# Reordering one step of a hand-scheduled pipeline: later multiply-adds, an earlier seed, the sigmoid at the front

## The chip, the core and the metric

The kernel runs on one core of a Trainium2 chip. The metric is the device time of one execution in microseconds. Most executions of one kernel agree within 0.3%; where a ratio to the kernel before is given, the runs of both were made on the same chip in the same rounds. Two experiments set side by side can come from different rounds.

## The reference, cut to what matters

```python
X = np.fft.fft(x, axis=1)                 # x: (8, 3136, 256)
X = np.fft.fft(X, axis=2).real            # the attention block
h = np.maximum(X @ w_in, 0.0)             # w_in: (256, 1024)
conv = sum(conv_w[k] * shifted(h, k) for k in range(3))   # along the sequence; cut
out = (h * 1 / (1 + np.exp(-conv))) @ w_out               # w_out: (1024, 256)
```

The kernel turns the Fourier transform into matrix products with tables and uses symmetry, so that the columns of one half of a sequence give both halves. While one batch goes through the second part ("the steps"), the next batch's transform runs beside it, cut into pieces and hung on the steps.

## The kernel before

The second part has 8 batches × 4 chunks of columns × 8 blocks of 128 features = 256 steps. The matrix products write tiles in PSUM, the other tiles of a step lie in SBUF; both are memories of the core. One step's parts, with the engine on which each runs:

```python
def seed(s):                      # ScalarE: pa starts from a scaled row
    pa[s] = psa.tile(...)         # 2 PSUM buffers
    act(pa[s][:, 0:n], eb[b, c], AF.Copy, scale=ge[:, f:f + 1])

def products(s):                  # TensorE
    pb[s] = psb.tile(...)         # 1 PSUM buffer
    mm(pb[s][:, 0:n], G[0:P - 1, 1, fs], PQ[b][1][...], True, True)
    mm(pa[s][:, 0:n], G[:, 0, fs], PQ[b][0][...], False, True)

def combine(s):                   # twice: ScalarE copies pb scaled by 1 or -1, VectorE adds it to pa
    ...
        act(nb[:, i, cols], p[:, cols], AF.Copy, scale=-1.0 if i else 1.0)        # L485
        nc.vector._custom_dve(TENSOR_ADD_SAT, out=to, in0=a[:, cols],             # L486
                              in1=nb[:, i, cols], s0=BIG, s1=0.0)

def first_tap(s):                 # ScalarE, L492
    act(gs[s], hs[s][:, 0:n], AF.Copy, scale=cw[:, 0, s[2]:s[2] + 1])

def other_taps(s):                # VectorE, L498: two multiply-adds
    for k in (1, 2):
        stt(out=g, in0=h[:, k:k + n], scalar=cw[:, k, f:f + 1], in1=g, op0=ALU.mult, op1=ALU.add)

def sigmoid(s):                   # ScalarE, L501
    act(gs[s], gs[s], AF.Sigmoid)

def gate(s):                      # half GpSimd (L508), half VectorE (L509)
    m = n // 2
    gt(g[:, m:n], g[:, m:n], h[:, m + 1:n + 1], op=ALU.mult)
    vt(g[:, 0:m], g[:, 0:m], h[:, 1:m + 1], op=ALU.mult)
```

The schedule is written by hand. Every engine is given its own instructions in the order in which this loop issues them:

```python
LAG = 3
for t in range(n + LAG):
    run("act")                    # copies of the next batch's transform
    if t < n:
        products(steps[t])
        combine(steps[t])
    if 0 <= t - 2 < n:
        gate(steps[t - 2])
    run("load")
    if 0 <= t - 1 < n:
        sigmoid(steps[t - 1])
    run("dve")                    # the next batch's transform on VectorE
    if t < n:
        first_tap(steps[t])
        other_taps(steps[t])
    if t + 1 < n:
        seed(steps[t + 1])
    if t >= LAG:
        mm2(steps[t - LAG])       # TensorE; every eighth step also the output copies on ScalarE
    run("pe")
```

## Time and profile before

| | kernel before |
|---|---|
| median of the runs | 1336.1 us |
| TensorE / VectorE / ScalarE / GpSimd busy | 91% / 88% / 66% / 35% |

Two engines are near their limits, and the work of a step goes round between four engines. Such a profile is read from the timeline of one step: for each idle stretch, which instruction ended it, and what stood in front of that instruction on its own engine. The prediction below shows those lines. In lines of the profile PE is TensorE (PEld its loading of weights), DVE is VectorE, ACT ScalarE and POOL GpSimd, and L158 is line 158 of the kernel.

### The profile page before, as it was taken

The page shows a single profiled execution, that of the slowest core. Times are in us where ns is not written, and L with a number is a line of the kernel's source. Part 1 is how long each engine was busy: PE and PEld are TensorE (multiplying, and loading weights), DVE is VectorE, ACT ScalarE, POOL GpSimd, SP SyncE. Part 2 cuts the span into 40 slices and gives each one's busy share as a digit, 9 for nine tenths or more (in the row PEclk, how much of TensorE's full clock was granted, in tenths as well). Part 3 has the DMA queues.
Part 4 walks back from the last instruction along what each step waited for, and adds up shares of the span by engine and source line. Part 5 has one row for each costly group of instructions (what it writes and reads, how often), then busy time and mean ns, then how long its engine had stood idle before and what let it go on. Part 6 is the DMA issues. An engine that isn't in the chain of part 4 may idle for free.

```text
span 1334.3 us, 15340 instructions
## 1 busy us (share of the span) xinstructions
PE 1214.4 (91%) x4914; PEld 892.2 (67%) x4914; DVE 1175.9 (88%) x1664; ACT 887.0 (66%) x1558; POOL 462.1 (35%) x507
## 2 busy tenths in 40 slices
PE   0748899989899999999999999999999999999998
PEld 0425677767676777777676777767677777776766
DVE  6969999998998999998999899999899888878885
ACT  0225666667666677776767777776777767777775
POOL 2415525242532435242523335242332223222222
PEclk9968999999999999999999999999999999999999
DMA  7601202021120102120102102120001000100001
GB/s 227 176 25 37 85 25 65 32 64 35 54 67 24 52 26 71 49 75 25 60 13 74 50 25 73 48 75 0 25 24 48 27 24 25 34 30 22 24 20 43
DMA packets 46840, 66.02 MB, mean 49 GB/s; under 512 B 5600, under 2 KB 35196, under 8 KB 46504
## 3 DMA queue, kind: packets, MB, share of 16 engines
q1 hardware_dynamic: 41012, 49.80, 11.8%
q0 software_dynamic: 5120, 12.85, 3.2%
q10 hardware_dynamic: 628, 2.40, 0.6%
q8 instruction: 38, 0.62, 0.2%
q14 instruction: 42, 0.34, 0.1%
HBM read 39.24 MB, written 25.74 MB: 49 GB/s over the span
## 4 chain that ended last, share of the span: by engine, by line
DVE 50%; PE 22%; ACT 12%; issue 12%; DMA 3%; POOL 1%; DVEq 0%; ACTq 0%; POOLq 0%; SPq 0%
DVE g L498 16%; DVE h L486 15%; PE po L89 11%; ACT g L492 6%; PE pd L89 4%; DVE g L509 4%; PE pa L89 4%; PE pb L89 4%; DVE xh L158 3%; ACT os L525 2%; DVE xh L147 2%; DVE w L174 2%; DMA out_dram<-os 1%; ACT nb L485 1%; ACT pa L466 1%
## 5 line engine op out<-in xcount | busy, mean ns | idle before, releaser
L89 PE MATMUL po<-wout,g 128*128 128x256 f32 (+2 forms) x3200 | 735.9, 380 | 0.7 <-POOL g L508 0.7
L89 PEld LDWEIGHTS po<-wout,g 128*128 128x128 f32 (+2 forms) x3200 | 602.9, 188 | 149.1 <-issue 19.0
L498 DVE SCALAR_TENSOR_TENSOR g<-h,cw,g 128x770 f32<-128x770 f32 (+2 forms) x512 | 537.1, 1049 | 82.0 <-ACT g L492 72.3
L508 POOL TENSOR_TENSOR g<-g,h 128x385 f32<-128x385 f32 (+1 forms) x256 | 295.0, 1152 | 776.9 <-ACT g L501 634.1
L485 ACT ACTIVATE nb<-pb 128x386 f32<-128x386 f32 (+4 forms) x512 | 227.6, 499 | 147.2 <-PE pb L89 145.8
L501 ACT ACTIVATE g<-g 128x770 f32<-128x770 f32 (+2 forms) x256 | 221.1, 864 | 149.1 <-DVE g L498 148.6
L486 DVE CUSTOM_DVE_ANT_0 h<-pa,nb 128x386 f32<-128x386 f32 (+4 forms) x512 | 265.7, 561 | 50.4 <-PE pa L89 31.9
L492 ACT ACTIVATE g<-h,cw 128x770 f32<-128x770 f32 (+2 forms) x256 | 243.6, 952 | 46.9 <-DVE h L486 30.3
L89 PE MATMUL pa<-pt,G 128*128 128x386 f32 (+2 forms) x512 | 223.7, 518 | 43.8 <-ACT pa L466 43.6
L89 PE MATMUL pb<-qt,G 127*128 127x386 f32 (+2 forms) x512 | 215.8, 502 | 1.6 <-ACT nb L485 1.5
L89 PEld LDWEIGHTS pa<-pt,G 128*128 128x128 f32 x512 | 91.0, 191 | 144.7 <-ACT pa L466 101.4
L509 DVE TENSOR_TENSOR g<-g,h 128x385 f32<-128x385 f32 (+2 forms) x256 | 155.0, 606 | 0.5 <-ACT g L501 0.5
L466 ACT ACTIVATE pa<-eb,ge 128x386 f32<-128x386 f32 (+2 forms) x256 | 146.9, 574 | 8.1 <-DMA eb<-ed 8.1
L89 PE MATMUL pd<-tab,w 99*128 99x196 f32 (+2 forms) x448 | 123.1, 381 | 17.7 <-ACT g L492 6.1
L89 PEld LDWEIGHTS pb<-qt,G 127*128 127x128 f32 x512 | 94.7, 192 | 27.6 <-issue 4.5
L89 PEld LDWEIGHTS pd<-tab,w 99*128 99x128 f32 (+1 forms) x448 | 80.0, 189 | 44.7 <-ACT g L492 24.2
L122 POOL DMA_INDIRECT xh<-in_x_dram,idx x64 | 85.3, 1333 | 16.4 <-issue 12.2
L525 ACT COPY os<-po 128x256 f32<-128x256 f32 (+2 forms) x200 | 58.4, 384 | 13.5 <-DMA out_dram<-os 8.8
L158 DVE TENSOR_TENSOR xh<-xh 98x1024 f32<-98x1024 f32 (+1 forms) x32 | 51.1, 1603 | 0.1
L147 DVE TENSOR_TENSOR xh<-xh 98x1020 f32<-98x1020 f32 (+1 forms) x32 | 46.6, 1466 | 0.0
L89 PE MATMUL po<-win,dm 128*128 128x512 f32 x8 | 5.7, 872 | 38.9 <-DMA dm<-dft_dim_dram 38.9
L174 DVE TENSOR_TENSOR w<-xh 98x508 f32<-98x508 f32 (+1 forms) x32 | 37.5, 1172 | 0.1
(84 smaller groups left out, 352.8 us busy)
## 6 DMA issues: line engine op xcount, KB each, us to landing
out_dram<-os SPq DMA_DIRECT2D x184, 128.0 KB
xh<-in_x_dram SPq DMA_DIRECT2D x16, 784.0 KB
eb<-ed SPq DMA_DIRECT2D x16, 193.0 KB
tab<-dft_seq_dram SPq DMA_DIRECT2D x4, 601.8 KB
raw<-in_moe_w_in_dram ACTq DMA_DIRECT2D x2, 1024.0 KB
raw<-in_moe_w_out_dram SPq DMA_DIRECT2D x1, 2048.0 KB
eb<-ed SPq DMA_DIRECT2D x8, 209.0 KB
eb<-ed SPq DMA_DIRECT2D x8, 192.5 KB
```

Source lines behind the costliest of these rows:

```text
L89: nc.tensor.matmul(o, l, r, start=start, stop=stop, skip_group_check=True)
L122: nc.gpsimd.indirect_dma_start(out=xh[b, h][0:NP, 4 + m].rearrange("p q d -> p (q d)"), out_offset=None, in_=bass.AP(tensor=x.tensor, offs ...
L158: vt(flat(to, to + 2), flat(0, 2), flat(2, 4), op=op)
L466: act(pa[s][:, 0:n], eb[b, c], AF.Copy, scale=ge[:, f:f + 1])
L485: act(nb[:, i, cols], p[:, cols], AF.Copy, scale=-1.0 if i else 1.0)
L486: nc.vector._custom_dve(TENSOR_ADD_SAT, out=to, in0=a[:, cols], in1=nb[:, i, cols], s0=BIG, s1=0.0)
L492: act(gs[s], hs[s][:, 0:n], AF.Copy, scale=cw[:, 0, s[2]:s[2] + 1])
L498: stt(out=g, in0=h[:, k:k + n], scalar=cw[:, k, f:f + 1], in1=g, op0=ALU.mult, op1=ALU.add)
L501: act(gs[s], gs[s], AF.Sigmoid)
L508: gt(g[:, m:n], g[:, m:n], h[:, m + 1:n + 1], op=ALU.mult)
L509: vt(g[:, 0:m], g[:, 0:m], h[:, 1:m + 1], op=ALU.mult)
L525: nc.scalar.copy(out=osb[0:m, j % 2], in_=pt[0:m, j % 2])
```

## The change

The intent is to take the wait for the first tap off VectorE: the multiply-adds of a step are put off to the next step, when their tap is long done. The sigmoid then comes a step later too, and the change puts it at the very front of the step.

```diff
         run("act")
+        if 0 <= t - 2 < n:
+            sigmoid(steps[t - 2])
         if t < n:
             products(steps[t])
             combine(steps[t])
+        if t + 1 < n:
+            seed(steps[t + 1])
+        if t < n:
+            first_tap(steps[t])
         if 0 <= t - 2 < n:
             gate(steps[t - 2])
         run("load")
+        run("dve")
         if 0 <= t - 1 < n:
-            sigmoid(steps[t - 1])
-        run("dve")
-        if t < n:
-            first_tap(steps[t])
-            other_taps(steps[t])
-        if t + 1 < n:
-            seed(steps[t + 1])
+            other_taps(steps[t - 1])
         if t >= LAG:
             mm2(steps[t - LAG])
```

## The prediction

> **What bounds the kernel now.** The kernel computes 256 steps: 8 batches, 4 chunks of columns, 8 blocks of features. One step t makes `products` (TensorE), `combine` (ScalarE scales and copies `pb` into `nb`, VectorE adds it to `pa`, twice), `first_tap` (ScalarE), two multiply-adds `other_taps` (VectorE), and, in later steps, `sigmoid` (ScalarE), `gate` (half VectorE, half GpSimd) and `mm2` (TensorE). The schedule is written by hand: each engine takes its instructions in the order of the text, so what matters is who waits for whom around one step. I read the busy shares first, then the work of each engine in stretches, then VectorE's list of waits, then the timeline of one step.
>
> The page's busy shares, and the windows (first data row: batches 0 to 6 with their transform of the next batch beside them; second: the last batch alone):
>
> ```profile
> PE 1214.4 (91%) x4914; PEld 892.2 (67%) x4914; DVE 1175.9 (88%) x1664; ACT 887.0 (66%) x1558; POOL 462.1 (35%) x507
> ```
>
> ```profile
> core 0: us, PE busy (x) PEld busy (x) DVE busy (x) ACT busy (x) POOL busy (x), PEclk, DMA share, GB/s
> 90.40:1186.00 1095.60, 1038.03 (x4216) 765.66 (x4215) 997.07 (x1385) 764.47 (x1344) 396.09 (x424) 0.99 0.14 43
> 1186.00:1318.50 132.50, 129.74 (x512) 94.07 (x512) 108.91 (x156) 104.05 (x181) 36.04 (x37) 1.00 0.08 25
> ```
>
> TensorE and VectorE run near their limits together. The first add of the steps starts at 90.4 us and the last step's at 1318.5, so 255 steps take 1228.1 us, 4.82 each; VectorE is busy for 997.07 + 108.91 = 1106.0 of it and idle for 122.1, or 0.48 a step. No rearrangement of VectorE's waits can therefore gain more than 122 us (9%), and TensorE, with 1167.8 of the 1228.1 busy, would stop it well before. VectorE's waits, in the list of who waited for whom:
>
> ```profile
> DVE g L498 <- ACT g L492: 72.3, 119, 0.9
> DVE h L486 <- PE pa L89: 31.9, 45, 9.6
> DVE h L486 <- ACT nb L485: 18.0, 25, 2.1
> ```
>
> The change aims at the first: multiply-adds (L498) waiting for the first tap (L492). The timeline of one undisturbed step of the last batch, VectorE and then ScalarE (start, duration, instruction, idle before):
>
> ```profile
> 1212.09 1.02 DVE L498 SCALAR_TENSOR_TENSOR g<-h,cw,g 128x769 f32<-128x769 f32 x1
> 1213.03 1.02 DVE L486 CUSTOM_DVE_ANT_0 h<-pa,nb 128x385 f32<-128x385 f32 x2
> 1213.96 0.55 DVE L509 TENSOR_TENSOR g<-g,h 128x384 f32<-128x384 f32 x1
> 1215.11 2.08 DVE L498 SCALAR_TENSOR_TENSOR g<-h,cw,g 128x769 f32<-128x769 f32 x2 [0.60 <-ACT g L492]
> 1217.11 0.55 DVE L486 CUSTOM_DVE_ANT_0 h<-pa,nb 128x385 f32<-128x385 f32 x1
> ```
>
> ```profile
> 1213.15 0.85 ACT L501 ACTIVATE g<-g 128x769 f32<-128x769 f32 x1 [0.64 <-DVE g L498]
> 1214.14 0.94 ACT L492 ACTIVATE g<-h,cw 128x769 f32<-128x769 f32 x1
> 1214.98 0.57 ACT L466 ACTIVATE pa<-eb,ge 128x385 f32<-128x385 f32 x1
> 1215.71 0.87 ACT L485 ACTIVATE nb<-pb 128x385 f32<-128x385 f32 x2 [0.16 <-PE pb L89]
> 1217.22 0.85 ACT L501 ACTIVATE g<-g 128x769 f32<-128x769 f32 x1 [0.64 <-DVE g L498]
> ```
>
> The step is 1217.11 − 1213.03 = 4.08 us. Read the order on ScalarE: the two scaled copies (1215.71) come before the sigmoid (1217.22). So the next adds find `nb` ready and start the moment the multiply-adds end, while the sigmoid, which also waits for those multiply-adds, runs beside the adds. VectorE's only idle time is the 0.60 before the multiply-adds.
>
> **What the Trainium skill says.** "Perfetto Trace Analysis", section "Tensor Engine Instruction": "ACT/DVE/GPSIMD are strict FIFO". The trace agrees: the seed at 1214.98 reads only `eb` and `ge`, which had long been there, and still starts only behind the tap. "ScalarE: Activation LUTs", section "What ACT_TABLE_LOAD costs": an activation takes 186 ns + 0.833 ns an element, 93 more for a pointer operand, and neighbours overlap by about 93. For the sigmoid of 769 that gives 827 ns, against 850 here; tap and seed overlap by 1214.14 + 0.94 − 1214.98 = 0.10. The same page, section "Table sets: the hidden batching unit", says that cheap functions lie in every set. The by-shape groups agree: L501 has a single table load in the whole run, although copies and sigmoids alternate, so the moved sigmoid adds none.
>
> **The change part by part.** No instruction is added or removed; the same 256 of each kind are put in another order.
>
> *Multiply-adds one step later.* In step t VectorE now does adds(t), gate(t−2), transform work if there is some, multiply-adds(t−1). Their tap was made a step earlier, so the wait for it goes. In the step above the multiply-adds start at once behind the gate, 0.47 after its start (two neighbours on VectorE overlap by 0.08) in place of 1.15 (1215.11 − 1213.96): −0.68.
>
> *Sigmoid(t−2) first on ScalarE.* Its input is now the output of multiply-adds(t−2), which VectorE finishes as the **last** thing of step t−1. Behind it in the same FIFO stand the scaled copies of step t, without which VectorE can't start adds(t). This closes a ring: multiply-adds end → sigmoid → first scaled copy → adds. VectorE has nothing else to do in it. Its idle time each step, from this trace:
> - end of the multiply-adds to the start of a sigmoid: 1213.15 − 1213.11 = 0.04;
> - sigmoid 0.86 (page: 221.1 us over 256), less 0.10 overlap with the copy behind it: 0.76;
> - first scaled copy, mean of L485: 0.50;
> - its end to the add's start, where an add did wait for it: 0.03 to 0.13, say 0.10.
>
> Sum: 1.40 us. The undisturbed step becomes 0.93 (adds) + 0.47 (gate) + 2.08 (multiply-adds) + 1.40 = 4.88, up from 4.08.
>
> *Seed ahead of the tap.* It gets the `pa` products off earlier; nothing on VectorE waited for them except in the 31.9 us above, which the 1.40 swallows. The tap is behind it, but nobody needs it until the next step.
>
> *What the ring hides.* TensorE needs 1167.8 / 255 = 4.58 a step, and the second scaled copy frees `pb` early in the step, so it can run about one step ahead. ScalarE needs 868.5 / 255 = 3.4. Copies of transform results lie ahead of the sigmoid, but find ScalarE waiting anyway. Transform work on VectorE lies in the ring at its full length; the 1106.0 counts it.
>
> *The sum.* From the first add to the last: 1106.0 busy, plus about 14 because an add no longer overlaps a multiply-add (0.08 in some 170 steps), less 2 for the multiply-adds put off beyond the last add, plus 255 × 1.40 = 357: 1475. At the end of a chunk (32 times) six or seven output copies of 0.29 us spacing follow the tap. The tap ends about 3.5 into the step, so they end at 5.3 to 5.6, and the sigmoid behind them starts some 0.4 late where no transform work stretches the step: 32 × 0.4 ≈ 13. First add at 90.4, as now. Tail behind the last add: adds, gate, multiply-adds(254) 3.7; sigmoid and gate 1.5; multiply-adds(255) 2.2; sigmoid 0.9; GpSimd's gate 1.3; last `mm2` 3.2; last copy and store 3.4: 16 (it is 15.8 now). Total 90 + 1475 + 13 + 16 = 1594, call it **1595 us**, 19% slower.
>
> **The rivals.**
> 1. *The tap's wait goes and nothing takes its place: faster.* For it: 72.3 us of waits really vanish; were they all gained, 1263. Against it: TensorE has only 60 us free in the stretch, so about 1280 to 1300 at best, and the FIFO order puts the sigmoid ahead of `nb`. For this to hold the sigmoid's wait would have to be met before its turn; but its producer is VectorE's last instruction before the adds.
> 2. *The ring costs, but mostly beside TensorE's bound: the same, or up to 5% slower (1340 to 1400).* For it: many steps now last 4.8 to 5.5 because of TensorE, and the 0.48 idle a step are recovered. Against it: VectorE's 4.34 busy plus 1.40 is 5.74, above TensorE's 4.58 in every kind of step. The idle time already there is counted as recovered.
> 3. *TensorE also falls out of step: slower still (1640 to 1700).* Gates come late in the ring and `mm2` stands behind the next products. If products, `mm2` and transform matmuls (4.2 to 5.1 together) couldn't run ahead of the adds, their lateness would add to the 1.40. The second scaled copy ends about 1.8 into the step and then products of the next can start, nearly a whole step early; so I expect little.
>
> **Range and chances.** The 1.40 is uncertain by 0.1 a step (26 us), chunk ends and GpSimd's late gates by 15, so 1550 to 1635. The ring follows from the program's order and the FIFO, which leaves little for the rest: faster 0.01, the same 0.02, slower 0.97.
>
> **What would show it.** In the changed profile the wait of L498 for L492 should be gone; L486 should wait for `nb` (L485) some 250 times, about 1.4 us each, 330 to 370 us in all; the timeline should show multiply-adds, sigmoid, scaled copy, adds strictly one after another, an undisturbed step of 4.8 to 5.0, and TensorE's busy share near 76%. I am wrong if the adds start at the end of the multiply-adds as now, if the sigmoid's wait ends before them, or if the adds' wait is for `pa` from TensorE.

## More of the kernel before

One execution of the kernel before, among the first group of experiments, took 3246 us; it is in no ratio, and nothing here tells why it was slow.

One line that the prediction didn't use turned out to matter. It has the durations (minimum / median / maximum, in ns) of the transform's additions L158, here of the kernel before:

```profile
L158 DVE TENSOR_TENSOR xh<-xh x32: 1211/1886/1946, 37.0 to 1000.3; 98x1024 f32<-98x1024 f32 x16, 99x1024 f32<-99x1024 f32 x16
```

The same operation on 98 or 99 rows of 1024 takes 1.21 us at best and 1.89 us at the median. A spread like this suggests that something slows the instruction while it runs. I read only means from the groups when I predicted.

## The result, and the profile after

The changed kernel takes 1551.4 us (median of 4; 1549.5 to 1557.6). Its ratio to the kernel before is 1.161, with a 95% interval of 1.157 to 1.165. A ratio here is the mean time of one kernel's fast runs over that of the other's of the same rounds, so it isn't quite the ratio of the medians quoted. It is 16% slower.

The busy shares of the page, and the windows between the first add (92.3 us) and the last step's (1530.7 us), of the changed kernel:

```profile
PE 1282.9 (83%) x4914; PEld 915.3 (59%) x4914; DVE 1125.2 (73%) x1664; ACT 871.0 (56%) x1558; POOL 372.0 (24%) x507
```

```profile
92.30:1530.70 1438.40, 1234.54 (x4738) 882.06 (x4736) 1052.88 (x1538) 851.58 (x1523) 341.93 (x461) 0.96 0.11 35
```

VectorE is idle for 1438.4 − 1052.9 = 385.5 us of the stretch, up from 122.1 in the kernel before. It is also *busy* for 53 us less, with the same instructions but for two multiply-adds. GpSimd too has become quicker, by 90 us. VectorE's waits in the changed kernel (who waited for whom: us in total, times, longest):

```profile
DVE h L486 <- ACT nb L485: 325.4, 226, 2.8
DVE h L486 <- PE pa L89: 35.9, 15, 9.6
DVE h L486 <- PE po L89: 11.2, 8, 1.5
```

The wait of L498 for L492 is gone from the list, as intended, and a wait of the adds for their scaled copy has come, 226 times. The timeline of an undisturbed step of the last batch shows why, VectorE first and then ScalarE:

```profile
1399.80 1.02 DVE L498 SCALAR_TENSOR_TENSOR g<-h,cw,g 128x769 f32<-128x769 f32 x1
1402.20 1.02 DVE L486 CUSTOM_DVE_ANT_0 h<-pa,nb 128x385 f32<-128x385 f32 x2 [1.38 <-ACT nb L485]
1403.14 0.55 DVE L509 TENSOR_TENSOR g<-g,h 128x384 f32<-128x384 f32 x1
1403.60 2.07 DVE L498 SCALAR_TENSOR_TENSOR g<-h,cw,g 128x769 f32<-128x769 f32 x2
1407.05 1.02 DVE L486 CUSTOM_DVE_ANT_0 h<-pa,nb 128x385 f32<-128x385 f32 x2 [1.38 <-ACT nb L485]
```

```profile
1400.85 0.84 ACT L501 ACTIVATE g<-g 128x769 f32<-128x769 f32 x1 [1.17 <-DVE g L498]
1401.60 0.85 ACT L485 ACTIVATE nb<-pb 128x385 f32<-128x385 f32 x2
1402.34 0.59 ACT L466 ACTIVATE pa<-eb,ge 128x385 f32<-128x385 f32 x1
```

The multiply-adds end at 1399.80 + 1.02 = 1400.82. The sigmoid starts 0.03 later, the first scaled copy 0.75 after that, and the first add 0.60 later still. Nothing overlaps: while ScalarE runs sigmoid and copy, VectorE stands for 1.38 us; while VectorE works, ScalarE's sigmoid waits. In the kernel before the copies stood in front of the sigmoid, and the adds followed the multiply-adds without a gap. The step grows from 4.08 us to 1407.05 − 1402.20 = 4.85.

The other half of the result is what became *shorter*. The line view of L158 in the changed kernel:

```profile
L158 DVE TENSOR_TENSOR xh<-xh x32: 1207/1218/1226, 36.8 to 1160.8; 98x1024 f32<-98x1024 f32 x16, 99x1024 f32<-99x1024 f32 x16
```

The spread is gone: all 32 take about the former minimum. The groups between first and last add, before and after: L158 46.4 to 34.1 us, L147 41.9 to 33.8, L174 34.8 to 19.0, L162 16.6 to 9.6, VectorE's gate L509 153.3 to 144.8. That is 51.7 us less.

All of these but the gate itself come right behind VectorE's gate in the order of the program, and they read two operands from SBUF. L163 and L175, which come right behind L162 and L174, did not shrink (681 to 683 ns and 700 to 703). The GpSimd half of the gate is the candidate. Its place in the step has moved. In the kernel before it started at 1214.07 in the step shown in the prediction, 0.11 after VectorE's half, and ran beside what came next:

```profile
1214.07 1.16 POOL L508 TENSOR_TENSOR g<-g,h 128x385 f32<-128x385 f32 x1 [2.88 <-ACT g L501]
```

In the changed kernel it starts as soon as the sigmoid at the front of the step is done, when VectorE is still idle, and ends beside the adds:

```profile
1401.78 0.87 POOL L508 TENSOR_TENSOR g<-g,h 128x385 f32<-128x385 f32 x1 [3.96 <-ACT g L501]
```

The Trainium skill, "SBUF — State Buffer", section "Who interferes with whom", says: "A DVE instruction with two SBUF inputs contends with a GpSimd instruction that reads SBUF", and that one with at most one SBUF input, outside the two-port modes, doesn't. The adds read `pa` from PSUM and `nb` from SBUF; the transform's additions read both inputs from SBUF. The traces agree in both parts. Of the 28 L158 from the first add on, in the kernel before, the 8 that no GpSimd gate touched took 1.21 us each at the median, the 16 beside a gate and no other work of GpSimd 1.89, and the 4 beside other work too 1.92. Of the 512 adds 289 run beside a gate in the changed kernel and 66 in the kernel before; they take 563 ns on average and 561.

### The profile page after: what moved, and what is told of

Same layout as the page of the kernel before. It is cut to its first block, busy times and chain, and to the rows that moved or that the text cites. A ratio compares the mean times of both kernels' runs of the same rounds, so it can differ in the third digit from the quotient of the medians.

```text
span 1547.7 us, 15337 instructions
## 1 busy us (share of the span) xinstructions
PE 1282.9 (83%) x4914; PEld 915.3 (59%) x4914; DVE 1125.2 (73%) x1664; ACT 871.0 (56%) x1558; POOL 372.0 (24%) x507
## 4 chain that ended last, share of the span: by engine, by line
DVE 56%; ACT 20%; PE 12%; issue 3%; DMA 1%; DVEq 1%; SPq 0%; ACTq 0%; POOL 0%; POOLq 0%
DVE g L498 26%; DVE h L486 15%; ACT g L501 12%; DVE g L509 7%; ACT nb L485 6%; PE po L89 5%; PE pd L89 2%; PE pb L89 2%; PE pa L89 2%; DVE xh L158 2%; ACT os L525 2%; DVE xh L147 1%; DMA out_dram<-os 1%; DVE w L175 1%; DVE w L174 1%
## 5 line engine op out<-in xcount | busy, mean ns | idle before, releaser
L89 PE MATMUL po<-wout,g 128*128 128x256 f32 (+2 forms) x3200 | 755.7, 387 | 11.0 <-DVE g L509 3.9
L89 PEld LDWEIGHTS po<-wout,g 128*128 128x128 f32 (+2 forms) x3200 | 613.4, 193 | 182.4 <-DVE g L509 35.9
L486 DVE CUSTOM_DVE_ANT_0 h<-pa,nb 128x386 f32<-128x386 f32 (+4 forms) x512 | 266.9, 563 | 386.1 <-ACT nb L485 325.4
L498 DVE SCALAR_TENSOR_TENSOR g<-h,cw,g 128x770 f32<-128x770 f32 (+2 forms) x512 | 533.8, 1043 | 9.1
L508 POOL TENSOR_TENSOR g<-g,h 128x385 f32<-128x385 f32 (+1 forms) x256 | 229.3, 896 | 1096.7 <-ACT g L501 835.5
L89 PE MATMUL pb<-qt,G 127*128 127x386 f32 (+2 forms) x512 | 239.8, 551 | 83.8 <-ACT nb L485 82.5
L492 ACT ACTIVATE g<-h,cw 128x770 f32<-128x770 f32 (+2 forms) x256 | 243.6, 952 | 109.3 <-DVE h L486 109.0
L89 PE MATMUL pd<-tab,w 99*128 99x196 f32 (+2 forms) x448 | 130.6, 399 | 93.4 <-ACT g L492 41.1
L89 PEld LDWEIGHTS pa<-pt,G 128*128 128x128 f32 x512 | 103.8, 203 | 90.5 <-ACT pa L466 31.4
L509 DVE TENSOR_TENSOR g<-g,h 128x385 f32<-128x385 f32 (+2 forms) x256 | 146.5, 572 | 1.9 <-ACT g L501 1.9
L158 DVE TENSOR_TENSOR xh<-xh 98x1024 f32<-98x1024 f32 (+1 forms) x32 | 38.8, 1218 | 0.1
L147 DVE TENSOR_TENSOR xh<-xh 98x1020 f32<-98x1020 f32 (+1 forms) x32 | 38.5, 1212 | 0.0
L89 PE MATMUL pd<-tab,ea 98*1 98x197 f32 (+2 forms) x112 | 14.1, 335 | 18.7 <-DVE qt L261 18.7
```

What stands on the lines that cost most here:

```text
L89: nc.tensor.matmul(o, l, r, start=start, stop=stop, skip_group_check=True)
L158: vt(flat(to, to + 2), flat(0, 2), flat(2, 4), op=op)
```

## The experiments

The first theory (the ring): the changed kernel loses 1.38 us a step because sigmoid and scaled copy stand between the end of the multiply-adds and the adds that follow. Its rivals: the loss comes from the later multiply-adds, or from the seed's place. The second theory (contention): the gain of some 50 us within VectorE's instructions comes from the new place of GpSimd's gate. Its rival: those instructions are quicker because TensorE, DMAs and ScalarE are less busy. Means of transform groups below are, like those above, taken from the first add on.

### e1: the sigmoid back behind the scaled copies

```diff
-        if 0 <= t - 2 < n:
-            sigmoid(steps[t - 2])
         if t < n:
             products(steps[t])
             combine(steps[t])
+        if 0 <= t - 2 < n:
+            sigmoid(steps[t - 2])
```

> The changed kernel with only the sigmoid of two steps ago moved back behind the scaled copies of this step. Ring theory (the changed kernel loses 1.38 us a step because sigmoid and scaled copy stand between the multiply-adds and the next adds): VectorE's waits for nb fall from 325 us to under 60, and the time falls by at least 200 us, to 1350 or less. Rival (the loss comes from the multiply-adds being one step late, or from the seed ahead of the tap): both are still there, so the time stays within 3% of 1551. A second theory is put to the test beside it: instructions of VectorE that follow its gate directly are lengthened by up to 0.68 us while GpSimd runs its half of the gate. If so, the first multiply-add, which now follows the gate in most steps, rises and the mean of L498 goes from 1.04 to 1.2 or more, and the time is 1310 to 1350; without such contention L498 stays at 1.04 and the time is 1280 to 1300, bound by TensorE.

Measured: 1355.6 us (1349.2 to 1359.7; ratio to before 1.015, interval 1.009 to 1.020), some 196 us less than the changed kernel by moving one instruction. The adds' waits for `nb` are 7.1 us in all. The ring is shown as the cause; later multiply-adds and the seed's place were still there. The time is some 6 us above the expected limit, and the second theory says why: L498 has a mean of 1184 ns, short of the 1.2 us that I had set for it but far from 1.04. One undisturbed step of e1, of both engines:

```profile
1225.00 0.56 DVE L509 TENSOR_TENSOR g<-g,h 128x384 f32<-128x384 f32 x1
1225.04 1.24 POOL L508 TENSOR_TENSOR g<-g,h 128x385 f32<-128x385 f32 x1 [2.79 <-DVE h L486]
...
1225.47 2.68 DVE L498 SCALAR_TENSOR_TENSOR g<-h,cw,g 128x769 f32<-128x769 f32 x2
```

The pair of multiply-adds follows the gate directly and takes 2.68 us, where it took 2.08 in the kernel before. There, the wait for the tap had put it 0.60 later, when GpSimd was nearly done. So the 72 us "wait for the tap" in the kernel before were mostly no loss: all L498 together take 606.1 us in e1 and 537.1 before, 69 us more, and e1 isn't faster than the kernel before.

### e2: the kernel before, with the whole gate on VectorE

```diff
-        m = n // 2
-        gt(g[:, m:n], g[:, m:n], h[:, m + 1:n + 1], op=ALU.mult)
-        vt(g[:, 0:m], g[:, 0:m], h[:, 1:m + 1], op=ALU.mult)
+        vt(g, g, h[:, 1:n + 1], op=ALU.mult)
```

> The kernel before with the whole gate on VectorE, none of it on GpSimd. Contention theory (the transform's additions on VectorE took longer before because GpSimd's half of the gate ran beside them): the means fall to what the changed kernel shows, L158 from 1657 to about 1218 ns, L147 from 1503 to 1213, L174 from 1242 to 680, L162 from 1186 to 684. Rival (they are shorter in the changed kernel because TensorE, the DMAs or the activations are less busy there): they stay within 10% of before, since those are as busy here. Time: the gate gains 0.39 us a step on VectorE (100 us), contention gives back about 50, and part lies in the wait for the tap: 1336 to 1400.

Measured: 1335.8 us, ratio 1.000 (0.997 to 1.003). L158 has a mean of 1218 ns, L147 1216, L174 695, L162 684. The durations of L158, to be read against the line of the kernel before:

```profile
L158 DVE TENSOR_TENSOR xh<-xh x32: 1215/1218/1226, 36.3 to 996.2; 98x1024 f32<-98x1024 f32 x16, 99x1024 f32<-99x1024 f32 x16
```

TensorE, ScalarE and the DMA engines are as busy as before (91%, 67% and 14%, against 91%, 66% and 13%). So the contention is with GpSimd's gate and the rival falls. The gate itself now has a mean of 973 ns in place of 606, 94 us more in all, and the wait for the tap is down to 6.3 us, because the longer gate covers it. The 94 us cost nothing for two reasons: without the stalls VectorE is busy for only 48 us more (1223.6 against 1175.9 in the whole run), and it is idle for 51 us less.

### e3: the seed back behind the tap

```diff
-        if t + 1 < n:
-            seed(steps[t + 1])
         if t < n:
             first_tap(steps[t])
+        if t + 1 < n:
+            seed(steps[t + 1])
```

> The changed kernel with the seed put back behind the first tap, all else as changed. Ring theory: the seed is not in the ring, and the time stays at 1551, within 1%. Rival (the seed ahead of the tap delays the tap and so the end of the step): 1520 or less. Other rival (the seed's new place helps by letting TensorE run ahead): 1570 or more.

Measured: 1550.6 us, ratio to before 1.161, the same as the changed kernel. In this schedule, with the ring, the seed's place is worth nothing, either way.

### e5: half of the sigmoid out of the ring

```diff
-            sigmoid(steps[t - 2])
+            sigmoid(steps[t - 2], 1)      # GpSimd's half of the columns
         if t < n:
             products(steps[t])
             combine(steps[t])
+        if 0 <= t - 2 < n:
+            sigmoid(steps[t - 2], 0)      # VectorE's half
```

> The changed kernel with the sigmoid split by columns: the half that GpSimd gates stays ahead of the scaled copies, the half that VectorE gates goes behind them. Ring theory, as a dose: 385 elements fewer stand in the ring, an estimate of 0.32 to 0.33 us a step from the slope between the 386-column copy (0.49) and the 769-column sigmoid (0.85), so 1551 - 256 x 0.32 = 1469, and the usual wait for nb falls from 1.38 to about 1.06. Rival (VectorE waits because the multiply-adds, not the sigmoid's length, hold something else back): the time doesn't follow the length, 1540 to 1560. The transform's additions stay at 1218 and 680 ns, since GpSimd's half still runs beside the adds.

Measured: 1474.7 us (ratio 1.104). The usual wait is 1.06, as the timeline of VectorE shows:

```profile
1354.51 1.03 DVE L486 CUSTOM_DVE_ANT_0 h<-pa,nb 128x386 f32<-128x386 f32 x2 [1.06 <-ACT nb L485]
```

The loss follows the length of what stands in the ring: 0.32 us a step out of it gave 77 us back, against 82 expected. The expectation's working doesn't give its 0.32, though: the slope that it names, 0.36 us over 383 elements, makes 0.36 for 385, so 92 us. The sigmoid's own half settles the size: it takes 0.53 us and the whole 0.85, 0.32 less. The transform's additions stay at 1218 and 682 ns.

### e4 and e6: no gate on GpSimd, or a quarter of it

These two have e1's order. e4 has e2's gate besides; e6 has this:

```diff
-        m = n // 2
+        m = 3 * n // 4
```

> The sigmoid behind the scaled copies (as e1) and the whole gate on VectorE (as e2). Contention theory: beside no gate on GpSimd the multiply-adds return from 1184 to 1045 ns and the transform's additions to 1218 and 680, so VectorE needs 1106 - 55 + 101 = 1152 us between first and last add, as in e2, and has lost its wait for the tap. If that wait still counted, the time is 1290 to 1320. Rival (in e2 the longer gate already covers the wait for the tap, which is 6 us there, and the give and take with TensorE sets the time): 1325 to 1340, like e2 and the kernel before.

> As e1, but GpSimd gates a quarter of the columns in place of half. Contention theory: GpSimd's part is done at about the time VectorE's is, so the instruction behind the gate hardly waits: L498 between 1040 and 1080 ns (1184 in e1), L158 under 1350. VectorE needs about 0.2 us a step less than in e4. Time 1290 to 1325, the best of all. Rival (what lengthens them is any beginning of an instruction beside GpSimd, whatever the length of its part): L498 stays at 1150 or more and the time at 1345 to 1360.

Measured: e4 1328.9 us, ratio 0.995 (0.994 to 0.997), as the rival had it; e6 1343.9 us, ratio 1.007 (1.006 to 1.009). In e4 L498 is back at 1044 ns and VectorE is still busy for nearly all of the stretch. In e6 L498 is at 1103 ns, which neither expectation had, and L158 at 1373, slightly over the limit that I had set. What e6 does tell is how the stall grows. A step of e6:

```profile
1225.27 0.76 DVE L509 TENSOR_TENSOR g<-g,h 128x576 f32<-128x576 f32 x1
1225.31 1.10 POOL L508 TENSOR_TENSOR g<-g,h 128x193 f32<-128x193 f32 x1 [2.79 <-ACT g L501]
1225.94 2.34 DVE L498 SCALAR_TENSOR_TENSOR g<-h,cw,g 128x769 f32<-128x769 f32 x2
```

A pair of multiply-adds right behind the gate takes 2.07 us with no gate on GpSimd (e4), 2.34 with 193 columns (e6) and 2.68 with 385 (e1): 0.27 and 0.61 us more. What counts is how long GpSimd's gate still runs when the pair starts. In e6 that is 1225.31 + 1.10 − 1225.94 = 0.47, in e1 1225.04 + 1.24 − 1225.47 = 0.81; the pair loses 0.20 less than that in both. My idea that a quarter would be done before VectorE's own part was wrong: beside VectorE's gate those 193 columns took 1.10 us on GpSimd.

### e7: a schedule built from both findings

The copies stay ahead of the sigmoid, so there is no ring. GpSimd's half of the sigmoid comes first; VectorE starts the step with its half of the gate of the step before's columns, so that the adds fall where GpSimd's gate runs; `mm2` comes one step later.

```diff
-    LAG = 3
+    LAG = 4
...
         run("act")
-        if 0 <= t - 2 < n:
-            sigmoid(steps[t - 2])
+        if 0 <= t - 3 < n:
+            gate_low(steps[t - 3])         # VectorE's half
         if t < n:
             products(steps[t])
             combine(steps[t])
+        if 0 <= t - 2 < n:
+            sigmoid(steps[t - 2], 1)
+            gate_high(steps[t - 2])        # GpSimd's half
+            sigmoid(steps[t - 2], 0)
...
-        if 0 <= t - 2 < n:
-            gate(steps[t - 2])
```

> A schedule built from both findings. The scaled copies stay ahead of the sigmoid (no ring). The sigmoid is in halves, GpSimd's half first, so that GpSimd's gate starts about 0.6 us after the multiply-adds end; VectorE starts the step with its own half of the gate of one step earlier (0.47 us) and then does the adds, so GpSimd's gate runs beside the adds, where the changed kernel showed no lengthening. mm2 comes one step later (lag 4). If both findings hold: no usual wait of VectorE for nb or for the tap, L498 back to about 1045 ns and L158 to about 1220 (against 1184 and 1533 in e1), VectorE busy for about 1060 to 1080 us between first and last add, TensorE the bound with 1168, and the time 1270 to 1315. If contention isn't what e1 suffered from, L498 stays near 1180 and the time near 1350. If TensorE's own waits set the time, contention goes and the time still stays at 1325 to 1340, as in e2 and e4.

Measured: 1276.3 us, correct, ratio 0.954 (0.953 to 0.956): faster than both kernels. The chain of work that ended last, followed back from the last instruction, was VectorE's for 50% of the span and TensorE's for 22% in the kernel before; it is now TensorE's:

```profile
PE 74%; DVE 15%; issue 4%; DMA 3%; ACT 2%; POOL 1%; SPq 0%; ACTq 0%; DVEq 0%; POOLq 0%
```

Contention went only in part: L498 has a mean of 1094 ns and L158 1464, not 1045 and 1220, and VectorE was busy for 1102 us of the 1172 from 90 to 1262. In a step of e7 the adds end at 1202.17 and GpSimd's gate at 1202.64, so it still stalls the multiply-adds that follow:

```profile
1201.77 0.87 POOL L509 TENSOR_TENSOR g<-g,h 128x385 f32<-128x385 f32 x1 [3.02 <-ACT g L503]
1202.08 2.44 DVE L498 SCALAR_TENSOR_TENSOR g<-h,cw,g 128x770 f32<-128x770 f32 x2
```

The gate runs for 0.56 beside the pair, and the pair takes 0.37 more than 2.07, 0.19 less than the 0.56: the size found in e6 and e1. The time came as expected, though less contention went than expected; four more runs take e7 apart.

### e8, e9, e10, e11: what helped e7

e8 is the kernel before, e9 is e4 and e10 is e1, each with this line alone:

```diff
-    LAG = 3
+    LAG = 4
```

> The kernel before with mm2 one step later (lag 4 in place of 3) and nothing else. e7 changed two things at once: where the gate runs, and this. If the later mm2 is what helped e7, this one is 1275 to 1310. If the order of gate and adds is what helped, the time stays within 1% of 1336: in the profile before, TensorE hardly waits for a gate (0.7 us), but for the seed (43.6 us), and the lag moves no seed.

> e4 (sigmoid behind the scaled copies, whole gate on VectorE) with lag 4. TensorE waited little for gates in e4 (1.5 us for matmuls, 11.3 for weight loads), so by the order theory 1320 to 1332; if the later mm2 is what helped e7, 1270 to 1300.

> e1 (sigmoid behind the scaled copies, GpSimd's gate running into the multiply-adds) with lag 4. e7 differs from this by the halved sigmoid and by the place of VectorE's half of the gate alone. In e1 TensorE waited 10 us for GpSimd's gate, which goes. Order and contention theory: L498 stays near 1184 ns and the time at 1335 to 1355. Lag theory: 1280 to 1300.

Measured: e8 1350.4 us (ratio 1.011), e9 1338.2 (1.002), e10 1366.0 (1.023). The later `mm2` costs about 10 us each time, 14, 9 and 10 against the kernel before, e4 and e1, and helps none.

e11 is e9 with the whole gate on VectorE at the front of the step:

```diff
+        if 0 <= t - 3 < n:
+            gate(steps[t - 3])
         if t < n:
             products(steps[t])
             combine(steps[t])
         if 0 <= t - 2 < n:
             sigmoid(steps[t - 2])
...
-        if 0 <= t - 2 < n:
-            gate(steps[t - 2])
```

> e9 (copies first, whole gate on VectorE, lag 4) with the gate moved from behind the adds to the beginning of the step, of the step before's columns. It has e7's place of the gate without GpSimd and without halves. If the place of the gate is what helped e7 (it fills the time in which the adds would wait for nb or pa), the time falls from e9's 1338 to 1275-1300 although VectorE has about 0.39 us a step more to do than without GpSimd's half relieved. If what helped is that GpSimd's half runs beside the adds without lengthening anything, the time stays within 1% of 1338.

Measured: 1292.6 us, ratio 0.967 (0.965 to 0.969). The place of the gate alone, without GpSimd and without halves, gives 46 of the 62 us between e9 and e7; the remaining 16 come with GpSimd's half beside the adds and the halved sigmoid together, which no run separates. The traces of e9 and e11 account for most of the 46: VectorE's idle time before the adds falls from 72.0 to 47.1 us, as it must if the gate fills time in which they would wait for `pa` or `nb`, and its busy time falls from 1226.3 to 1210.2 us, because neighbours overlap more in the new order.

## Why the prediction was right

The time, 1551.4 us, lies in the range of 1550 to 1635, and the direction was forecast with 0.97. The mechanism is the one foretold. That the time lies in the range is partly luck: it is 1.4 us above the lower edge, two of the four runs (1549.5) are below it, and nothing in the range stood for the term that was mis-sized. By its steps:

- **The tap's wait goes.** It did: 72.3 us to none. The gain of 0.68 a step behind the gate is there; the multiply-adds start 1403.60 − 1403.14 = 0.46 behind the gate's start. It is a gain only because GpSimd's gate had moved away: e1 has the same early start and pays it back in stalls.
- **The ring of 1.40 us.** It measured 1.38 (0.03 + 0.75 + 0.60), and e1 and e5 show that it is the cause and that it is worth what it is long. The adds waited for `nb` 226 times, for 325.4 us in all, a little under the 250 times and 330 to 370 us expected. The sigmoid's term in the sum was the trace's 0.86; the 827 ns worked out from the skill's figures was an estimate and is in no sum.
- **The undisturbed step.** 4.88 expected, 4.85 measured.
- **"Transform work on VectorE lies in the ring at its full length; the 1106.0 counts it."** This is the term that was mis-sized. I expected VectorE to be busy for 1106 + 14 − 2 = 1118 us between first and last add; it was 1052.9. Of the 65 us, 52 are the five groups listed above, made shorter because GpSimd's gate moved out of their way, and 4 more are L498 itself (534.9 to 528.8 us, two instructions fewer). The other 9 are in the overlap of neighbours, of which I expected to lose 14 and which shrank by 4 (94.7 to 90.3 us): the multiply-adds that had waited for the tap, 119 times, now overlap the gate, by some 0.08 each. I took the durations of the kernel before as constants of the instructions, although the change moved another engine beneath them. e2 shows that they weren't.
- **Chunk ends.** 357 + 13 = 370 us of idle time expected, 385.5 measured. The small waits for `pa` and others that I took as swallowed weren't quite.
- **The ends.** First add at 92.3 in place of 90; tail of 1547.7 − 1530.7 = 17.0 in place of 16.
- **The sum.** 1594 − 65 + 15 + 2 + 1 = 1547, the span of the profiled run.

Rival 1 (faster) failed where the prediction said, at the place of the sigmoid in ScalarE's order: e1 undoes that and is 1.5% slower than before, not faster, since the tap's wait was hiding contention. Rival 2 (the same, or up to 5% slower, because TensorE's bound hides the ring) failed too: a step lasts 1438.4 / 255 = 5.64 us, and TensorE is idle for 1438.4 − 1234.5 = 204 us of the stretch, up from 60. Rival 3 (TensorE out of step) didn't come about: the adds' waits on TensorE are 35.9 + 11.2 us, and those on it before were 31.9.

One reading missed: TensorE's busy share, 83% where I said 76%. The same 4914 matmuls are recorded with 1282.9 us in place of 1214.4, while the mean clock granted to TensorE in the profiled run is 0.952 of full speed against 0.984. The clock isn't all of it: in the last batch, where both traces show 1.00, a matmul counts 2.6% more than before (148.57 us over 571 from 1360 to 1530.7 us, against 125.74 over 496 from 1190 to 1318.5). The runs don't settle what makes that part; TensorE isn't in the ring, and the time doesn't hang on it.

## What to carry to other kernels

Before an instruction is moved ahead on an in-order engine, look at who makes its input, and whether that producer's engine needs something that stands behind the moved instruction: if so, the two engines take turns and the whole length between them is lost in every round. A duration in a profile can belong to that schedule and not to the instruction: look at minimum and median, and where they differ, ask which other engine ran beside. And a wait that looks like the largest gain may be covering something; here the wait for the tap kept the multiply-adds clear of GpSimd, and taking it away (e1) gained nothing.

## What the Trainium skill lacked or had wrong

- "SBUF — State Buffer", section "Who interferes with whom", has the rule that explains most of the 52 us, and no measured size for it with two-input instructions. Here a pair of multiply-adds right behind VectorE's gate takes 2.07 us alone, 2.34 when GpSimd's gate still runs for 0.47 and 2.68 when it runs for 0.81. L174 has a mean of 680 ns clear of GpSimd's gate and of 1242 in the kernel before.
- The same section says that the order of issue decides who blocks. The traces agree, and show a chain that it doesn't spell out: in the step of the prediction VectorE's gate began 0.11 us before GpSimd's and took its usual 0.55, GpSimd's took 1.16 in place of 0.87, and where VectorE's next instruction follows at once (e1), the stall falls on that one.
- "Perfetto Trace Analysis", section "Identifying the Most-Contended Engine", takes VectorE's occupancy as a fair measure of its distance from the roofline. Here some 43 of its 1106 busy us (4%) were stalls inside four groups of the transform's instructions, as e2 shows by taking GpSimd's gate away.
